# A spectral mixing block and a SwiGLU block in one kernel: which queues store the result, and in what pieces

## The chip, the cores and the metric

The kernel runs on one core of one Trainium2 chip. The metric is the device time of one execution in microseconds (us). Differences of about 0.3% are what a measurement of this kernel can tell from no change. All data are 32-bit floats.

## The reference

```python
batch, seq, dim = (8, 3008, 256)
X = np.fft.rfft(x, axis=1)
Y = X * (filt_r + 1j * filt_i)[None, :, :]
y = np.fft.irfft(Y, n=x.shape[1], axis=1)

x = y.reshape(B * S, D)                  # 24064 tokens of 256
g = x @ w_gate                           # 256 -> 1536
silu = g * (1.0 / (1.0 + np.exp(-g)))
val = x @ w_val
return silu * val @ w_out                # 1536 -> 256
```

The first block filters each channel along the sequence in the frequency domain. The second is a gated feed-forward network on every token. The weights come as 64-bit floats, which the kernel converts itself.

## The kernel before, in words

**Spectral block.** The Fourier transform of length 3008 = 47 x 64 is done as matrix products in two stages forward (`stage1`, and `stage2a` with the filter) and two back (`stage2b`, `stage3`). Intermediate results go through DRAM (`d1`, `d2`) and come back in another layout. The spectral work on batch b+1 runs in between the feed-forward work on batch b, in small pieces. Its tables, filters and inputs are loaded into a shared tile called `lent` and into tiles called `t4` (`t` in the profile). The matrix products are `pa`, `pb`, `pc` and `pd` by stage.

**Feed-forward block.** A batch is worked on in four chunks k = 0 to 3. The hidden units are split in three groups g = 0 to 2. One pair (k, g) is a step, a `Group` object, and takes about 25 us. The products use fewer multiplications than plain block products: a Toom-like scheme for the hidden layer (tokens P, Q, A, B, E, products `wk`, `wa`, `we`) and a Strassen-like scheme for the projection. The projection reads seven combinations of the hidden tiles `h`; four are made by GpSimd as sums (tokens S00 to S31, `h<-h` in the profile). GpSimd also makes differences such as D01 (`D<-f,f`), which VectorE combines further into the operands of later products (line 884, `wa<-wk,D`).

**Order of work.** One string, `SCHEDULE` (line 88), lists the tokens of a step in program order, and every engine and every queue executes its share in that order. A prime after a token means that it belongs to the step before, or, for projections and stores, to the one before that. The tokens `x0.o'` to `x5.o'` are the stores of a finished chunk. They stand at the beginning of a step, between S00/S01 and D01. The last chunk has a list of its own, `LAST` (line 99).

**The output tile.** The projection of a chunk is summed over the three groups in a tile `outs[b, k]` of 128 partitions, 16 rows and 96 columns, of which 94 hold data (`NR`); the two others are set to zero by GpSimd (line 824), so that VectorE can transpose whole 32 x 32 blocks (tokens z0 to z3, line 930). A chunk is then stored in twelve transfers (line 940), two to each token x0 to x5, each of up to 32 partitions with 16 pieces of 32 floats (128 bytes). SyncE's queue does this; in the last chunk SyncE and ScalarE take turns.

**The first batch.** Its first three chunks are taken in turns: all three with group 0, then with group 1, then with group 2, because the weights are still being converted (`takes_turns`, `order_of`). The tile of sums is therefore put away in DRAM (`o_dram`, line 935) after each of the first two groups and fetched again by `new_outs` (line 826); both move only the 94 columns with data. That is twelve transfers. The first batch also keeps and fetches `y` and its sums (`y_dram`, `yt_dram`), and stores and reloads the converted weights (`w_all`, lines 403 and 407).

**Queues.** Nearly all transfers are issued from SyncE's queue, in program order; ScalarE issues the stores of the spectral stages and half of the last chunk. GpSimd's queue issues no transfer.

Of the kernel before, what the change touches and what calls it, by code (L numbers as in the profile page):

```python
# [41 lines left out]
FP32 = mybir.dt.float32  # L42
# [6 lines left out]
B, S, C = 8, 3008, 256  # L49
# [6 lines left out]
NR = 2 * N1  # L56
NK = 4 * NS

NH = 4
# [3 lines left out]
RP = 96  # L63
NT = 3
NG = 3
# [31 lines left out]
KS = (-1, 0, 1, 2)  # L97

LAST = """
S00 S01 S10 S11 W1 o1 W2 o2 z0.o S20 S21 S30 S31 W6 o6 W5 o5 W3 o3 z1.o W7 o7 z3.o W4 o4 z2.o x0.o  # L100
x1.o x2.o x3.o x4.o x5.o
""".split()
BLOCKS = (0, 1, 3, 2)
PAIRS = ((0, 1), (1, 2), (2, 3), (0, 2), (1, 3), (0, 3))
# [68 lines left out]
def kernel(  # L173
# [10 lines left out]
    nc = tc.nc  # L184
# [9 lines left out]
    def pool(name, bufs, space=None):  # L194
        kw = {} if space is None else {"space": space}
        return ctx.enter_context(tc.tile_pool(name=name, bufs=bufs, **kw))
# [6 lines left out]
    wdpool = pool("wdram", 1, DRAM)  # L203
# [24 lines left out]
                  for i in range(4)]  # L228
    yt_dram = [wdpool.tile([128, 3 * len(PAIRS), TQ], FP32, name=f"yt_{k}") for k in range(NT)]
    y_dram = [wdpool.tile([128, 8, TQ], FP32, name=f"y_{k}") for k in range(NCHUNK)]  # L230
    o_dram = [wdpool.tile([128, 4 * NH, NR], FP32, name=f"o_{k}") for k in range(NT)]
    w_dram = wdpool.tile([NG, 128, NPR, 2, 128], FP32, name="w_all")
    wo_t = cpool.tile([128, NJ, 7, 128], FP32)

# [18 lines left out]
    pin = tc.keep_in_program_order  # L253

    def add(eng, dst, a, b):
        return eng.tensor_tensor(out=dst, in0=a, in1=b, op=ALU.add)  # L256
# [559 lines left out]
    outs = {}  # L816

    def takes_turns(b, k):
        return b == 0 and k < NT

    def new_outs(b, k, g):
        outs[b, k] = opool.tile([128, 4 * NH, RP], FP32, name=f"o_{b}_{k}_{g}", tag="o", bufs=2)
        if g == NG - 1 or not takes_turns(b, k):
            pin(nc.gpsimd.memset(outs[b, k][:, :, NR:], 0.0))
        if g:
            pin(nc.sync.dma_start(out=outs[b, k][:, :, 0:NR], in_=o_dram[k]))

    class Group:

# [93 lines left out]
        def project(self, op, last=False):  # L923

            b, k, q = self.b, self.k, self.g
            kind, p = op[0], int(op[1])
            if kind == "z":
                if q == NG - 1:
                    t = self.part(p)
                    pin(nc.vector.transpose(out=t, in_=t))  # L930
                return
            if kind == "x":
                t = outs[b, k]
                if q < NG - 1 and takes_turns(b, k) and p == 5:
                    pin(nc.sync.dma_start(out=o_dram[k], in_=t[:, :, 0:NR]))
                if q == NG - 1:
                    for n, (u, cq) in enumerate(divmod(m, 4) for m in (2 * p, 2 * p + 1)):
                        rows = min(32, NR - 32 * u)
                        at = (b * S + 32 * 32 * u + 2 * NH * k) * C + 32 * cq
                        pin(((nc.sync, nc.scalar)[n] if last else nc.sync).dma_start(  # L940
                            out=bass.AP(tensor=out.tensor, offset=out.offset + at,
                                        ap=[[32 * C, rows], [128, 4 * NH], [1, 32]]),
                            in_=t[32 * cq:32 * cq + rows, :, ts(u, 32)]))
                return
            at = {1: "A", 6: "A", 7: "A", 4: "A", 2: "F", 5: "G", 3: "G"}[p]
            if kind == "W":
                start = p in (1, 2, 5)
                if start:
                    self.bank(at, 3)
                for i in range(JB):  # L950
                    pin(nc.tensor.matmul(  # L951
                        out=self.tiles[at], lhsT=wo_t[:, JB * q + i, WO[p], :],
                        rhs=self.hs[i][:, HID[p]], start=start and i == 0,
                        stop=True, skip_group_check=True))
                return
            if q == 0 and p == 1:
                new_outs(b, k, q)
            i, cb = {1: (0, 0), 2: (0, 0), 6: (0, 1), 3: (0, 1), 4: (1, 0), 7: (1, 1),
                     5: (1, 1)}[p]
            dst = self.part(2 * i + cb)[:, :, 0:NR].rearrange("p n (t r) -> p t n r", t=2)  # L960
            src = self.tiles[at].rearrange("p (t n r) -> p t n r", t=2, n=NH)
            if q == 0 and at == "A":
                pin(nc.scalar.copy(out=dst, in_=src))
            else:
                pin(add(nc.vector, dst, dst, src))
# [7 lines left out]
    x0 = [t[0:NR, 8 * C * i:8 * C * i + 8 * C] for t, i in ((wo_f, 0), (wo_f, 1), (y_f, 0))]  # L973
    x0 = [t.rearrange("p (n c) -> p n c", c=C) for t in x0]
# [6 lines left out]
    with tc.tile_pool(name="start", bufs=1) as spool0:  # L981
# [12 lines left out]
        n = 0  # L994
# [68 lines left out]
        for p in ("A13", "A01"):  # L1063
            at = SLOT[p]
# [32 lines left out]
    def order_of(b):  # L1097

        steps = [divmod(step, NG) for step in range(NCHUNK * NG)]
        if b == 0:  # L1100
            steps[:NT * NG] = [(k, g) for g in range(NG) for k in range(NT)]
        return steps
# [39 lines left out]
    for step in range(NT, NT * NG):  # L1142
        chore(step, "Q3", lambda s: new_outs(0, *order_of(0)[s]), step)
# [4 lines left out]
    for b in range(B):  # L1148
# [36 lines left out]
        for step in range(NCHUNK * NG + (b == B - 1)):  # L1185
            ghost = step == NCHUNK * NG
            k, g = order_of(b)[min(step, NCHUNK * NG - 1)]
# [13 lines left out]
            last = ghost or b == B - 1 and step == NCHUNK * NG - 1  # L1201
            for place, token in enumerate(SCHEDULE):
# [5 lines left out]
                if op[0] == "t":  # L1208
                    n = int(op[1])
# [64 lines left out]
```

## Time and profile before

| | |
|---|---|
| time, median of three runs | 2918.26 us (2918.22 to 2924.73) |
| span of the profiled run | 2917.1 us |
| TensorE busy | 2850.2 us, 98% |
| VectorE busy | 2076.3 us, 71% |
| GpSimd busy | 1496.4 us, 51% |
| mean granted TensorE clock | 0.993 |
| stores to the result | 378 on SyncE's queue (first at 338.4 us), 6 on ScalarE's |
| kept sums, `o<-o` | 12 transfers, 752 KB each |

In the profile, PE is TensorE's matrix products, PEld its weight loads, DVE is VectorE, ACT ScalarE, POOL GpSimd, SP SyncE. "SPq" and "ACTq" are the queues on which SyncE and ScalarE issue transfers; the duration of such a line is that of the issues, not of the movement of data. A line of the timeline gives the start, the time, the engine, the line of code, the operation, the output and the inputs, and in square brackets the engine's idle time before it and what ended that. A line of the waits gives the waiting engine and its line, what it waited for, and then the total in us, the number of waits and the longest.

### The profile page before, as it was taken

The numbers are of one execution on the slowest core, as the hardware profiler recorded it, in microseconds if no ns is written. First come the engines' busy times: TensorE is split into PE (matmuls) and PEld (weight loads), VectorE is DVE, ScalarE is ACT, GpSimd is POOL, SyncE is SP. The second block draws the span as 40 slices with busy tenths as digits, with TensorE's granted clock in tenths as the row PEclk, the third lists the DMA queues.
The fourth block names the chain that finished last, engine by engine and source line by source line (L and its number), as shares of the span: only waits on it lengthen the run. The fifth ranks groups of instructions, "written<-read, shape, count | busy, mean of one in ns | idle before, by whom it ended". The sixth has DMA issues, their size and how long they took to land.

```text
span 2917.1 us, 47274 instructions
## 1 busy us (share of the span) xinstructions
PE 2850.2 (98%) x14784; PEld 2442.6 (84%) x14784; DVE 2076.3 (71%) x4664; ACT 1575.8 (54%) x4190; POOL 1496.4 (51%) x1613
## 2 busy tenths in 40 slices
PE   7999798999999999999999999999999999999998
PEld 6777687888888888888888888888888888888886
DVE  6888566767777676777677777676777776766666
ACT  6775344555555555555555555555555555555553
POOL 4876344545454545454544464545464545455442
PEclk9999999999999999999999999999999999999999
DMA  8799865666666766566656676566665666645443
GB/s 228 205 258 254 233 197 167 191 202 197 185 195 185 214 198 194 176 190 219 190 182 197 183 220 194 181 197 179 205 200 186 193 191 205 205 142 159 147 137 80
DMA packets 444350, 558.68 MB, mean 192 GB/s; under 512 B 251475, under 2 KB 346981, under 8 KB 444101
## 3 DMA queue, kind: packets, MB, share of 16 engines
q1 hardware_dynamic: 415349, 509.81, 59.1%
q10 hardware_dynamic: 28752, 45.85, 4.7%
q8 instruction: 120, 1.97, 0.3%
q14 instruction: 129, 1.06, 0.1%
HBM read 460.28 MB, written 95.24 MB: 190 GB/s over the span
## 4 chain that ended last, share of the span: by engine, by line
PE 86%; DVE 1%; DMA 1%; issue 0%; SPq 0%; DVEq 0%
PE wa L862 23%; PE wA L951 15%; PE wk L862 15%; PE we L862 12%; PE wG L951 8%; PE wF L951 3%; PE pd L765 3%; PE pc L731 2%; PE pb L698 2%; PE pa L639 1%; PE pa L641 1%; DMA t<-d 0%; DVE o L256 0%; DMA wt_t<-w_all 0%; DVE lent L714 0%
## 5 line engine op out<-in xcount | busy, mean ns | idle before, releaser
L862 PE MATMUL wa<-y_t,wt_t 128*128 128x188 f32 x4464 | 881.7, 324 | 6.8 <-DVE lent L714 1.7
L862 PEld LDWEIGHTS wa<-y_t,wt_t 128*128 128x128 f32 x4464 | 751.7, 191 | 87.5 <-ACT wa L888 9.1
L256 POOL TENSOR_TENSOR h<-h 128x376 f32<-128x376 f32 x190 | 184.5, 992 | 791.7 <-DVE h L909 791.7
L862 PEld LDWEIGHTS wk<-y,wt_t 128*128 128x128 f32 x2976 | 502.2, 190 | 79.9 <-DVE y L256 0.5
L862 PE MATMUL wk<-y,wt_t 128*128 128x188 f32 x2976 | 566.3, 323 | 0.0
L259 POOL TENSOR_TENSOR h<-h 128x376 f32<-128x376 f32 x570 | 563.3, 1010 | 0.0
L951 PE MATMUL wA<-h,wo_t 128*128 128x376 f32 x1536 | 548.8, 480 | 2.3 <-DVE o L256 1.6
L862 PE MATMUL we<-y_t,wt_t 128*128 128x188 f32 x2232 | 433.6, 324 | 0.8 <-ACT we L893 0.7
L259 DVE TENSOR_TENSOR we<-we,m 128x376 f32<-128x376 f32 x576 | 316.6, 554 | 142.7 <-PE we L862 94.0
L862 PEld LDWEIGHTS we<-y_t,wt_t 128*128 128x128 f32 x2232 | 371.3, 191 | 1.4 <-ACT we L893 1.0
L951 PEld LDWEIGHTS wA<-h,wo_t 128*128 128x128 f32 x1536 | 280.5, 190 | 106.5 <-DVE o L256 2.8
L259 POOL TENSOR_TENSOR D<-f,f 128x376 f32<-128x376 f32 x288 | 280.9, 987 | 149.4 <-ACT f L877 140.6
L897 ACT COPY m<-wa 128x376 f32<-128x376 f32 x576 | 271.7, 472 | 86.3 <-PE wa L862 83.3
L263 DVE SCALAR_TENSOR_TENSOR y<-wk,c 128x376 f32<-128x376 f32 x480 | 243.7, 540 | 84.9 <-ACT we L893 56.8
L904 ACT ACTIVATE u<-we 128x188 f32<-128x188 f32 x576 | 188.7, 328 | 190.0 <-DVE we L259 170.3
L904 ACT ACTIVATE g<-wa 128x188 f32<-128x188 f32 x576 | 187.3, 326 | 169.4 <-PE wa L862 153.4
L951 PE MATMUL wG<-h,wo_t 128*128 128x376 f32 x768 | 274.2, 479 | 1.2 <-DVE o L256 1.2
L877 ACT ACTIVATE f<-wk 128x376 f32<-128x376 f32 x288 | 139.2, 483 | 225.5 <-PE wk L862 159.5
L884 DVE SCALAR_TENSOR_TENSOR x<-wk,f 128x376 f32<-128x376 f32 x192 | 104.2, 543 | 214.0 <-PE wk L862 211.9
L881 ACT COPY c<-wk 128x376 f32<-128x376 f32 x288 | 136.0, 472 | 217.9 <-PE wk L862 217.9
L893 ACT COPY we<-y 128x376 f32<-128x376 f32 x480 | 221.2, 479 | 37.9 <-DVE h L909 24.7
L909 DVE TENSOR_TENSOR h<-wa,g 128x188 f32<-128x188 f32 x576 | 196.7, 345 | 34.3 <-ACT g L904 33.4
(156 smaller groups left out, 3822.1 us busy)
## 6 DMA issues: line engine op xcount, KB each, us to landing
wt_t<-w_all SPq DMA_DIRECT2D x174, 896.0 KB
wt_t<-w_all SPq DMA_DIRECT2D x174, 768.0 KB
lent<-later_tbl SPq DMA_DIRECT2D x84, 256.0 KB
lent<-in_filt_r_dram SPq DMA_DIRECT2D x336, 64.0 KB
d<-lent ACTq DMA_DIRECT2D x84, 256.0 KB
d<-t ACTq DMA_DIRECT2D x78, 240.0 KB
lent<-d SPq DMA_DIRECT2D x144, 128.0 KB
out_dram<-o SPq DMA_DIRECT2D x252, 64.0 KB
```

The source lines that it names most:

```text
L256: return eng.tensor_tensor(out=dst, in0=a, in1=b, op=ALU.add)
L259: return eng.tensor_tensor(out=dst, in0=a, in1=b, op=ALU.subtract)
L263: return nc.vector.scalar_tensor_tensor(out=dst, in0=a, scalar=-1.0, in1=b, op0=ALU.mult, op1=ALU.subtract)
L862: pin(nc.tensor.matmul(out=ps[:, z], lhsT=self.wt[:, SLOT[p], z], rhs=rhs, start=start and z == 0, stop=True, skip_group_check=True))
L877: pin(act.mul(self.small(f"f{i}", f"f{i}", 1), t[f"k{i}"], -1.0))
L881: pin(act.copy(out=self.small(f"c{i}", f"c{i}", 1), in_=t[f"k{i}"]))
L884: pin(v.scalar_tensor_tensor(out=dst, in0=t[f"k{j}"], scalar=-1.0, in1=t[f"f{i}" if j == 3 else f"D{at}"], op0=ALU.mult, op1=ALU.add))
L893: pin(act.copy(out=self.bank(f"e{at}"), in_=t[f"y{at}"]))
L897: pin(act.copy(out=self.small(f"m{at}", "m", 4), in_=t[f"a{at}"]))
L904: pin(act.activation(out=self.small(op, "g", 3, 1)[:, 0], in_=ps[:, 1], func=AF.Silu))
L909: pin(v.tensor_tensor(out=dst, in0=ps[:, 0], in1=g, op=ALU.mult))
L951: pin(nc.tensor.matmul(out=self.tiles[at], lhsT=wo_t[:, JB * q + i, WO[p], :], rhs=self.hs[i][:, HID[p]], start=start and i == 0, stop=Tru ...
```

## The change

It has three parts, all about moving the result. First, the stores of the first batch's chunks (b = 0) are issued from GpSimd's queue instead of SyncE's, so that SyncE's queue is left to the loads. Second, the sums that are put away between groups are moved as whole tiles of 96 columns, so that each partition is one contiguous piece in DRAM and in SBUF; the zero columns are then set once, at group 0, and travel with the tile. Third, the last chunk of all is stored in two halves: tokens x store the rows of the first half as soon as it is transposed, tokens X those of the second half at the end, and the transfers are dealt to SyncE, ScalarE and GpSimd in turn.

```diff
 LAST = """
-S00 S01 S10 S11 W1 o1 W2 o2 z0.o S20 S21 S30 S31 W6 o6 W5 o5 W3 o3 z1.o W7 o7 z3.o W4 o4 z2.o x0.o
-x1.o x2.o x3.o x4.o x5.o
+S00 S01 S10 S11 W1 o1 W2 o2 z0.o S20 S21 S30 S31 W6 o6 W5 o5 W3 o3 z1.o x0.o x1.o x2.o x3.o x4.o
+x5.o W7 o7 z3.o W4 o4 z2.o X0.o X1.o X2.o X3.o X4.o X5.o
 """.split()
...
-    o_dram = [wdpool.tile([128, 4 * NH, NR], FP32, name=f"o_{k}") for k in range(NT)]
+    o_dram = [wdpool.tile([128, 4 * NH, RP], FP32, name=f"o_{k}") for k in range(NT)]
...
-        if g == NG - 1 or not takes_turns(b, k):
+        if g:
+            pin(nc.sync.dma_start(out=outs[b, k], in_=o_dram[k]))
+        else:
             pin(nc.gpsimd.memset(outs[b, k][:, :, NR:], 0.0))
-        if g:
-            pin(nc.sync.dma_start(out=outs[b, k][:, :, 0:NR], in_=o_dram[k]))
...
-            if kind == "x":
-                t = outs[b, k]
+            if kind in "xX":
+                t, first, count = outs[b, k], 2 * NH * (kind == "X"), 2 * NH if last else 4 * NH
                 if q < NG - 1 and takes_turns(b, k) and p == 5:
-                    pin(nc.sync.dma_start(out=o_dram[k], in_=t[:, :, 0:NR]))
+                    pin(nc.sync.dma_start(out=o_dram[k], in_=t))
                 if q == NG - 1:
                     for n, (u, cq) in enumerate(divmod(m, 4) for m in (2 * p, 2 * p + 1)):
                         rows = min(32, NR - 32 * u)
-                        at = (b * S + 32 * 32 * u + 2 * NH * k) * C + 32 * cq
-                        pin(((nc.sync, nc.scalar)[n] if last else nc.sync).dma_start(
+                        at = (b * S + 32 * 32 * u + 2 * NH * k) * C + 128 * first + 32 * cq
+                        queue = nc.sync if b else nc.gpsimd
+                        if last:
+                            queue = (nc.sync, nc.scalar, nc.gpsimd)[(2 * p + n) % 3]
+                        pin(queue.dma_start(
                             out=bass.AP(tensor=out.tensor, offset=out.offset + at,
-                                        ap=[[32 * C, rows], [128, 4 * NH], [1, 32]]),
-                            in_=t[32 * cq:32 * cq + rows, :, ts(u, 32)]))
+                                        ap=[[32 * C, rows], [128, count], [1, 32]]),
+                            in_=t[32 * cq:32 * cq + rows, first:first + count, ts(u, 32)]))
```

## The prediction, made before the changed kernel was timed

> **What bounds the kernel now.** I read the page's head first, then busy time by stretches, then TensorE's waits, then the timeline of one step of the first batch and of the end.
>
> ```profile
> span 2917.1 us, 47274 instructions
> PE 2850.2 (98%) x14784; PEld 2442.6 (84%) x14784; DVE 2076.3 (71%) x4664; ACT 1575.8 (54%) x4190; POOL 1496.4 (51%) x1613
> ```
>
> TensorE sets the time. What can be gained lies where it is idle, and the stretches show where:
>
> ```profile
> 300.00:400.00 100.00, 85.35 (x409) 72.35 (x409) 66.73 (x143) 40.98 (x111) 44.98 (x47) 0.93 0.81 225
> 400.00:500.00 100.00, 87.19 (x435) 75.18 (x434) 58.64 (x133) 43.68 (x118) 43.10 (x45) 0.93 0.55 167
> 500.00:600.00 100.00, 100.00 (x524) 86.39 (x523) 71.97 (x164) 55.36 (x148) 45.89 (x48) 1.00 0.63 190
> ```
>
> The columns are the stretch, its length, and the busy time of PE, PEld, DVE, ACT and POOL, then granted clock, DMA share and GB/s. From 500 us to 2890 us TensorE is idle for 2 us in all. From 300 to 500 us it is idle for 14.65 + 12.81 = 27.5 us, and its clock records there hold 27.3 us at half speed, so 13.7 us more. About 41 us are to be had there. What ends the idle time:
>
> ```profile
> PE pb L698 <- DMA lent<-d: 11.9, 5, 8.4
> ...
> PE pd L765 <- DMA t<-d: 9.9, 1, 9.9
> ```
>
> These are loads on SyncE's queue. The timeline of the step that begins near 330 us (chunk 2, third group of hidden units) shows why one of them came late, and what GpSimd does meanwhile:
>
> ```profile
> 330.45 1.92 POOL L256 TENSOR_TENSOR h<-h 128x376 f32<-128x376 f32 x2 [11.20 <-DVE h L909]
> ...
> 336.20 0.99 POOL L259 TENSOR_TENSOR D<-f,f 128x376 f32<-128x376 f32 x1
> ...
> 338.38 10.12 SPq L940 DMA_DIRECT2D out_dram<-o  x12
> ...
> 339.25 0.55 DVE L884 SCALAR_TENSOR_TENSOR wa<-wk,D 128x376 f32<-128x376 f32 x1
> ...
> 352.56 0.37 SPq L407 DMA_DIRECT2D wt_t<-w_all  x1
> ...
> 359.59 0.39 SPq L530 DMA_DIRECT2D lent<-d  x1
> ...
> 362.48 2.05 PE L698 MATMUL pb<-lent 128*128 128x256 f32 x4 [8.43 <-DMA lent<-d]
> ```
>
> SyncE's queue issues the twelve stores of chunk 0 for 10.1 us; the weight reload and the load that TensorE waits for (the last line but one) stand behind them. In the built program a transfer on SyncE's or ScalarE's queue waits for the landing of the one eight places before it, so a slow one blocks all behind it. GpSimd makes the Strassen sums (`h<-h`) and then D01, which VectorE uses 2 us after it is done.
>
> ```profile
> 2909.45 0.58 DVE L930 STREAM_TRANSPOSE o<-o 128x384 f32<-128x384 f32 x1
> 2910.06 3.21 SPq L940 DMA_DIRECT2D out_dram<-o  x6
> 2910.06 3.34 ACTq L940 DMA_DIRECT2D out_dram<-o  x6
> ```
>
> At the end, all twelve stores wait for the last transpose; 7 us pass from there to the end of the span.
>
> **What the Trainium skill says.** "DMA: Bandwidth & Descriptors", SWDGE vs HWDGE vs iDMA: a DMA issued by GpSimd has its descriptors computed by cores of GpSimd itself. The trace before has none, so cannot agree or differ. The same page, Why small descriptors are slow: each packet carries a fixed overhead. The trace agrees: its 376-byte packets took 42 ns on average, its 6144-byte ones 298 ns, 7 times as long for 16 times the bytes. "TensorE: Matmul & The Clock Gate", What's actually happening: an idle window of about 3.4 us halves the clock. The trace agrees: after the idle 8.43 us it records half clock for 10.24 us, after 9.89 us again 10.24 us, after 2.76 us 3.41 us.
>
> **Part 1, stores of the first batch from GpSimd.** Removed: 48 issues from SyncE's queue (10.1, 10.3, 8.0 and 6.6 us of it in the steps of chunks 0 to 3) and 48 places in its chain of eight. Added: 48 issues on GpSimd, in its order. The built program shows where: behind the first sums `h<-h` come eight stores, a sum of the spectral stage, two stores, the second sums, two stores, and then D01. So D01 comes 12c later, c being one issue, and the second sums 10c later. The wait for the transposes costs nothing: z1 ends at 332.2 us, the first sums at 332.4 us.
>
> Who waits: VectorE for D01, and TensorE behind it. The room is best read in a step in which no DMA disturbs (chunk 3):
>
> ```profile
> 514.37 0.98 POOL L259 TENSOR_TENSOR D<-f,f 128x376 f32<-128x376 f32 x1 [0.88 <-ACT f L877]
> ...
> 517.86 0.54 DVE L884 SCALAR_TENSOR_TENSOR wa<-wk,D 128x376 f32<-128x376 f32 x1
> ...
> 520.36 1.44 PE L862 MATMUL wa<-y_t,wt_t 128*128 128x188 f32 x8
> ```
>
> D01 ends at 515.35 us, VectorE takes it 2.5 us later, its result is done at 518.40 us and TensorE reads it at 520.36 us, 2.0 us on. With the 0.88 us that GpSimd waited itself, 5.4 us; in the other steps 0.6 to 0.7 us of waiting, or none, and 2.0 to 2.6 us to VectorE. I take 5.0 us. The stall is 12c - 5.0 per chunk, four times.
>
> c is not in the trace. Lower end: SyncE's own issue of such a store, 0.48 us, or 0.62 us, which "SBUF — State Buffer" (A bandwidth-pool intuition that's wrong) gives for a GpSimd DMA alone; upper end 3.1 us, its price beside a VectorE copy that holds the port. The DMA page (Latency and other measured facts) has about 1 us to the first byte. Our stores have 512 pieces of 128 bytes; SyncE takes 0.48 us for one and 0.39 us for a load of 128 rows, 1.25 times less. I take 1.0 x 1.25 = 1.25 us, an estimate.
>
> Then a stall is 12 x 1.25 - 5.0 = 10.0 us, and four are 40.0 us. Such idle times cost half clock for 10.24 us, 5.1 us each: 20.5 us. Against this stand the 41 us of 300 to 500 us: with SyncE's queue free by 8 to 10 us and TensorE later by 10 us, the loads arrive before they are needed. The load for `pd` hangs partly on transfers that follow TensorE, so I leave 5 us of loss: -36.0 us. Part 1: 40.0 + 20.5 - 36.0 = +24.5 us.
>
> **Part 2, kept sums in whole tiles.** Twelve transfers (six out, six back) change from 2048 packets of 376 bytes to 128 of 6144: 12 x 2048 x 42 ns / 16 engines = 64.5 us become 12 x 128 x 298 ns / 16 = 28.6 us, 36 us less of DMA between 138 and 361 us. TensorE waits little for DMA before 300 us (1.4 us for x); the rest is in the 41 us already. The moved memsets (three of 0.13 us) lie in GpSimd's gaps, the padding columns add 2% to the bytes. I take -1.5 us.
>
> **Part 3, the last chunk in halves.** The first half's data are ready at 2906.6 us, before TensorE's last products, so its issues hide there. The second half then has four issues a queue instead of six: two of some 0.5 us fewer on SyncE and ScalarE, about -1.1 us. GpSimd has 8c for half the pieces, from 2906.6 us: at 1.0 us it issues until 2914.6 us, 1.2 us after today's last issue (2913.4 us), at 0.6 us earlier than the others. Between -1.2 and +2.5 us; I take -1.0 us.
>
> Sum: 24.5 - 1.5 - 1.0 = +22.0 us, 2940 us.
>
> **The rivals.** *Cheap issue, c = 0.62 us:* stalls of 2.4 us, 9.8 us in four, with 1.7 us of clock each 16.6 us; 16.6 - 36.0 - 2.5 = -22 us, 2896 us. For it: the published time for a DMA alone, SyncE's 0.48 us, and VectorE mostly reading PSUM here. Against: 512 pieces a store.
> *It cancels, c = 0.9 us:* stalls of 5.8 us, 23.2 us, clock 3.4 us each, 13.6 us; less 38.5 us makes -2 us, 2917 us. It needs c in a narrow band.
> *Dear issue, c = 2 us or more:* stalls of 19 us, 76 us, with clock 24 us, less 39 us: +61 us, 2979 us; with 3.1 us about 3032 us. For it: 512 pieces on two cores. Against: nothing in the trace; the published times are shorter.
>
> **How the numbers follow.** Forecast 0.40, cheap 0.33, cancels 0.17, dear 0.10. Faster by over 0.3% (8.8 us) is the cheap case, 0.33; within 0.3% the third, 0.17; slower the forecast and the dear case, 0.50. The range runs from 2894 us (the cheap case) to 2972 us (c near 1.8 us); outside are the dear case and a cheaper issue than I bound.
>
> **What would show it.** GpSimd's issues spaced by 1.25 us behind the first sums; TensorE waiting for VectorE or GpSimd some 10 us in the steps near 335, 380, 415 and 515 us, the last of them new in a stretch that was full; the 8.43 us and most of the 9.89 us wait gone; 6144-byte packets for the kept sums. It is wrong if GpSimd's issues are spaced under 0.9 us, if its sums run on while descriptors are made, or if the loads stay late with SyncE's queue free.

## The result, and the profile after

The changed kernel takes 2895.51 us (median of four runs, 2894.28 to 2897.16) against 2921.49 us before (the three runs of the table above and one more, 2925.41 us): a ratio of 0.9911, 95% interval 0.9894 to 0.9928. It was forecast to be 22 us slower; it is 26 us faster. Measured twice more, beside the experiments, the ratio was 0.9931 (0.9918 to 0.9943) and 0.9927 (0.9915 to 0.9940).

The head of the page of the changed kernel, and the same stretches as before:

```profile
span 2893.4 us, 47312 instructions
PE 2843.6 (98%) x14784; PEld 2434.4 (84%) x14784; DVE 2073.4 (72%) x4664; ACT 1576.6 (54%) x4190; POOL 1532.2 (53%) x1669
```

```profile
300.00:400.00 100.00, 91.17 (x451) 75.34 (x451) 71.04 (x155) 44.86 (x119) 65.04 (x77) 1.00 0.81 258
400.00:500.00 100.00, 95.24 (x497) 80.92 (x496) 63.60 (x150) 51.78 (x139) 59.94 (x69) 1.00 0.55 169
500.00:600.00 100.00, 100.00 (x530) 87.06 (x529) 71.78 (x166) 57.16 (x151) 43.93 (x46) 1.00 0.60 183
```

TensorE's idle time from 300 to 500 us has gone from 27.5 to 13.6 us, and the clock column reads 1.00 instead of 0.93: none of the 13.7 us that half clock cost is left. What is left of the waits has other causes. TensorE's waits from 300 to 500 us:

```profile
PE wa L862 <- DVE wa L884: 5.6, 4, 1.4
PE wA L954 <- POOL h L259: 4.6, 4, 2.5
...
PE pb L698 <- DMA lent<-d: 0.9, 1, 0.9
```

The waits of 8.43 and 9.89 us for loads are gone. The first two lines are new: four times TensorE waits for GpSimd's second sums, and four times for the operand that VectorE makes from D01, 10.2 us together. The timeline of the step of chunk 2, third group, shows the order that the prediction read from the built program:

```profile
323.92 5.34 POOL L943 DMA_DIRECT2D out_dram<-o  x8
...
330.49 1.41 POOL L943 DMA_DIRECT2D out_dram<-o  x2
331.92 1.95 POOL L259 TENSOR_TENSOR h<-h 128x376 f32<-128x376 f32 x2
...
332.96 1.86 PE L954 MATMUL wA<-h,wo_t 128*128 128x376 f32 x4 [0.38 <-POOL h L259]
...
335.21 0.99 POOL L259 TENSOR_TENSOR D<-f,f 128x376 f32<-128x376 f32 x1
...
336.85 1.54 PE L862 MATMUL wa<-y_t,wt_t 128*128 128x188 f32 x8 [1.39 <-DVE wa L884]
```

Eight issues take 5.34 us, 0.667 us each. The line of all stores on GpSimd's queue says the same (the shortest, the median and the longest issue in ns):

```profile
L943 POOL DMA_DIRECT2D out_dram<-o x56: 597/651/836, 323.9 to 2889.3; - x56
```

The eight issues at the end of the kernel, of 256 pieces each, are among the 56. The end of the kernel:

```profile
2883.79 5.27 SPq L943 DMA_DIRECT2D out_dram<-o  x8
2883.80 5.35 ACTq L943 DMA_DIRECT2D out_dram<-o  x8
...
2886.62 0.58 DVE L930 STREAM_TRANSPOSE o<-o 128x384 f32<-128x384 f32 x1
2887.49 2.43 POOL L943 DMA_DIRECT2D out_dram<-o  x4 [0.98 <-DVE o L930]
```

From the end of the last transpose to the end of the span it is 2893.4 - 2887.2 = 6.2 us; before it was 2917.1 - 2910.0 = 7.1 us.

**Where the time came from.** All of these kernels run the same 4653 arithmetic instructions and transposes on VectorE, and all but `e6_later` (in which 99 stand at other places) in the same order, so the start of one and the same instruction can be compared between two traces. The changed kernel's lead over the kernel before, by the time at which an instruction starts in the trace before (all times from the start of each trace's span):

| start before, us | 216 | 229 | 302 | 337 | 379 | 460 | 518 | 564 | 2753 |
|---|---|---|---|---|---|---|---|---|---|
| lead of the changed kernel, us | -0.2 | 1.5 | 3.0 | 8.7 | 17.5 | 25.7 | 21.1 | 22.9 | 22.8 |

The lead grows where the waits for loads were. It dips in the steps with stores on GpSimd (not in the table: 6.2 us at 353, 11.7 us at 393), and shrinks by 2.8 us for good in the step of chunk 3 (460 to 564 us), a stretch that was full before. It then stays to the end.

### The profile page after: what moved, and what is told of

Same layout as the page of the kernel before. It is cut to its first block, busy times and chain, and to the rows that moved or that the text cites. A ratio compares the mean times of both kernels' runs of the same rounds, so it can differ in the third digit from the quotient of the medians.

```text
span 2893.4 us, 47312 instructions
## 1 busy us (share of the span) xinstructions
PE 2843.6 (98%) x14784; PEld 2434.4 (84%) x14784; DVE 2073.4 (72%) x4664; ACT 1576.6 (54%) x4190; POOL 1532.2 (53%) x1669
## 4 chain that ended last, share of the span: by engine, by line
PE 89%; POOL 3%; DVE 2%; issue 1%; ACT 0%; DMA 0%; POOLq 0%; DVEq 0%
PE wa L862 24%; PE wA L954 16%; PE wk L862 15%; PE we L862 12%; PE wG L954 8%; PE wF L954 4%; PE pd L765 3%; PE pc L731 3%; PE pb L698 2%; PE pa L639 1%; PE pa L641 1%; POOL out_dram L943 1%; POOL h L259 1%; POOL h L256 0%; DVE o L256 0%
```

## The experiments

Theory A: the gain is part 1, SyncE's queue freed of the stores, and the prediction went wrong in the price of an issue on GpSimd and nothing else. Rival B: the gain is part 2, the shorter kept sums. Rival C: GpSimd's sums don't wait for its issues, so that these cost nothing at all. Each ratio below is against the kernel before on the same chip.

**Part 1 alone** (`e1_stores`).

```diff
-                        pin(((nc.sync, nc.scalar)[n] if last else nc.sync).dma_start(
+                        queue = nc.sync if b else nc.gpsimd
+                        pin(((nc.sync, nc.scalar)[n] if last else queue).dma_start(
```

> The kernel before with part 1 alone: the first batch's stores from GpSimd's queue. If the gain comes from SyncE's queue being free of the stores, nearly all of it is here: 0.992 to 0.994 of the time before (some 18 to 23 us less), GpSimd's issues spaced by 0.67 us as in the changed kernel, and the 8.4 and 9.9 us waits of TensorE gone. If the gain comes from the shorter transfers of the kept sums instead, this is within 8 us of the time before, or slower for the added issues on GpSimd.

2911.0 us, ratio 0.9965 (0.9953 to 0.9977): 10 us less, half of what theory A expected. An issue took 0.66 us. The long waits for loads are gone, as expected; but the trace is 6 us behind the kernel before at 229 us, where no store has run yet (one run; the run with part 3 alone, which has the same first batch as the kernel before, was 2.0 us behind there), and waits of up to 3.6 us for loads remain. TensorE's waits for them from 130 to 600 us:

```profile
PE pa L658 <- DMA x<-in_x_dram: 4.1, 2, 3.6
...
PE pb L698 <- DMA lent<-d: 3.6, 3, 1.5
```

**Part 2 alone** (`e2_sums`): the `o_dram`, `new_outs` and store lines of the change, nothing else.

> The kernel before with part 2 alone: kept sums as whole tiles. The prediction's share was -1.5 us; the two traces drift apart by about 3 us up to 320 us, before the first store, so I expect 2 to 4 us less and the waits at 354 and 441 us still there. The rival, that these transfers delayed the loads, expects 12 us or more.

2909.5 us, ratio 0.9963 (0.9951 to 0.9976): 11 us less, near the 12 us or more of rival B and far from the 2 to 4 us of theory A. Yet the long waits stand; TensorE's waits from 130 to 600 us in this run:

```profile
PE pd L765 <- DMA t<-d: 9.6, 1, 9.6
PE pb L698 <- DMA lent<-d: 9.3, 1, 9.3
```

So neither theory holds alone. The two parts gain about 10 us each by different waits: this trace gains 5.7 us on the kernel before from 302 to 337 us, where short waits and 3.4 us at half clock are gone, and stays near 8 us ahead from 353 us on.

**Part 3 alone** (`e3_tail`).

> The kernel before with part 3 alone: last chunk in two halves from three queues. From the last transpose to the end of the span it is 7.1 us before and 6.2 us in the changed kernel, so about 1 us less, 0.9997 of the time before. If GpSimd's issue at the end cost as much as 1.25 us, it would be 1 to 2 us more.

2919.38 us, ratio 0.9996 (0.9988 to 1.0004). The interval contains no change; the number is near the 0.9997 expected. The three ratios multiply to 0.9924, inside the interval of the whole change.

**Twice as many issues on GpSimd** (`e4_double`).

```diff
+                        parts = 1 if b else 2
+                        for h in range(parts):
+                            f, c = first + h * count // parts, count // parts
...
-                                ap=[[32 * C, rows], [128, count], [1, 32]]),
+                                            ap=[[32 * C, rows], [128, c], [1, 32]]),
```

> The changed kernel with each store of the first batch cut into two, so 24 issues on GpSimd for a chunk, of 256 pieces each (0.61 us an issue, as at the end of the changed kernel). If the prediction's sum was right but for the size of one issue, the delay is 24 x 0.61 = 14.6 us, the stall of TensorE 9 to 10 us a chunk instead of about 3, and half clock comes back: 30 to 45 us more than the changed kernel, 2925 to 2940 us. If GpSimd's sums don't wait for its issues, or have much more room than 5 us, it is within 5 us of the changed kernel.

2930.9 us, ratio 1.0035 (1.0023 to 1.0046): slower than before, and 35 us above the changed kernel's 2895.5 us; 4 us of that the profiled run had lost already at 130 us, before any store. Rival C falls. TensorE's waits from 300 to 600 us, and the step of chunk 2 in the timeline:

```profile
PE wA L957 <- POOL h L259: 28.5, 4, 8.0
```

```profile
328.11 9.42 POOL L946 DMA_DIRECT2D out_dram<-o  x16
337.55 1.27 POOL L256 TENSOR_TENSOR lent<-lent 128x512 f32<-128x512 f32 x1
338.75 2.50 POOL L946 DMA_DIRECT2D out_dram<-o  x4
341.27 1.92 POOL L259 TENSOR_TENSOR h<-h 128x376 f32<-128x376 f32 x2
342.31 2.87 PE L957 MATMUL wA<-h,wo_t 128*128 128x376 f32 x4 [6.67 <-POOL h L259]
```

Twenty issues stand ahead of the second sums, 9.42 + 2.50 = 11.9 us; TensorE waits 28.5 / 4 = 7.1 us a chunk for these sums, and another 3.9 us in all for the operand made from D01. Half clock is back: 37.5 us of it from 300 to 600 us, which costs 18.8 us. An issue of 256 pieces took 9.42 / 16 = 0.59 us against 0.667 us for 512.

**No stores of the first batch** (`e5_no_stores`); this kernel leaves the rows of batch 0 unwritten.

```diff
-                if q == NG - 1:
+                if q == NG - 1 and b:
```

> The changed kernel without the 48 stores of the first batch: the rows of batch 0 are not written, nothing else is left out. It shows what the stores still cost where they are. In the changed kernel TensorE waits 10.2 us for GpSimd's sums and for VectorE's operand made from D01 between 300 and 500 us, and falls back 2.8 us in the step of chunk 3. If these waits are the price of the issues, this is 8 to 13 us less than the changed kernel. If the waits for loads come back in their place, it is within 3 us of it.

2880.51 us, ratio 0.9874 (0.9861 to 0.9888), beside 0.9931 (0.9918 to 0.9943) for the changed kernel on the same chip: 16 us less by the medians, 13.9 us by the spans of the profiled runs (2879.3 and 2893.2 us). That is what the stores still cost in the changed kernel, 3.5 to 4 us a chunk. The stretches:

```profile
300.00:400.00 100.00, 97.63 (x495) 82.93 (x494) 78.77 (x169) 49.82 (x133) 56.00 (x57) 1.00 0.76 257
400.00:500.00 100.00, 100.00 (x535) 87.38 (x535) 68.50 (x163) 56.47 (x152) 41.27 (x44) 1.00 0.53 169
```

No wait for a load came back in place of those for GpSimd, but for the 1.1 us for `lent` that the changed kernel has too (0.9 us).

**All stores later in the step** (`e6_later`): tokens x0 to x5 behind S31 in `SCHEDULE`, for all batches.

```diff
-                ... S30' t1.2 x02 W7 S31' g13 y12 ...
+                ... S30' t1.2 x02 W7 S31' x0.o' x1.o' x2.o' x3.o' x4.o' x5.o' g13 y12 ...
-        chore(step, "Q3", lambda s: new_outs(0, *order_of(0)[s]), step)
+        chore(step, "E03", lambda s: new_outs(0, *order_of(0)[s]), step)
```

> The changed kernel with tokens x0 to x5 moved behind S31, where GpSimd has made all sums of the step, and with the fetch of the next tile of sums moved from Q3 to E03, so that SyncE doesn't stand waiting for these stores. If the remaining price is the place of the issues in GpSimd's order, it comes near the kernel without the stores: 6 to 12 us less than the changed kernel. The rival: the later stores hold the tile of sums or the loads, waits for transfers return, and nothing or less is gained.

2912.48 us, ratio 0.9983 (0.9975 to 0.9991): a miss as a kernel, but its trace is split in two. At 564 us its lead over the kernel before was 33.9 us (36.2 us without stores); at the end 10.0 us. It fell back 3 to 6 us at each of five places, near 875, 1230, 1579, 1938 and 2295 us of its own trace, in the later batches, where SyncE's stores had moved too. The trace shows what they held up. VectorE's waits from 600 to 2880 us have a line that the changed kernel's lack:

```profile
DVE paired L259 <- DMA x<-in_x_dram: 26.6, 8, 6.4
```

These are loads of the next batch's input on SyncE's queue. At four of the five places VectorE waits 5.3 to 6.4 us for one of them, and ScalarE and then TensorE wait behind VectorE, TensorE 2.7 to 3.6 us. How the moved stores made these loads late was not followed.

**Only the first batch's stores later** (`e8_first_later`): the same place on GpSimd for b = 0, the old place on SyncE for the others.

```diff
-        chore(step, "Q3", lambda s: new_outs(0, *order_of(0)[s]), step)
+        chore(step, "E03", lambda s: new_outs(0, *order_of(0)[s]), step)
...
+                    if old and op == "S31" and older is not None and older.b == 0:
+                        for p in range(6):
+                            older.project(f"r{p}.o")
```

> The changed kernel with the first batch's stores alone moved behind S31 on GpSimd, the other batches' stores left where they were, and the next tile of sums fetched at E03. The run with all stores moved kept pace with the kernel without stores up to 530 us and lost 24 us later, where SyncE's stores of the later batches had moved too. If that loss comes from the later batches, this one keeps the lead: 9 to 14 us less than the changed kernel, within 4 us of the kernel without stores. If not, it falls back as that run did.

2886.28 us (2881.88 to 2890.16), ratio 0.9898 (0.9883 to 0.9914), beside 0.9927 (0.9915 to 0.9940) for the changed kernel on the same chip: 9 us less. In the profiled runs it is 36.1 us ahead of the kernel before at 2753 us, as far as the kernel without stores, though it still makes the 48 transfers. That profiled run is the fastest of four; by the two ratios it is some 7 us short of the kernel without stores. TensorE's waits from 300 to 600 us hold nothing of the second sums or D01 any more:

```profile
PE pc L731 <- POOL lent L256: 1.7, 1, 1.7
PE pb L698 <- DMA lent<-d: 1.1, 1, 1.1
```

This version is faster than both kernels. The stores' place and that of the fetch changed together; no run has one without the other.

**The stores from ScalarE's queue** (`e7_scalar`): `nc.scalar` in place of `nc.gpsimd` for the first batch.

> The changed kernel with the first batch's stores from ScalarE's queue. These are again part of the chain of eight transfers, and ScalarE must issue them between its activations: 12 x 0.48 us a chunk if it never waits, more where the chain holds it. If the point of GpSimd's queue is that its transfers are outside the chain, this is 8 us or more slower than the changed kernel. If any queue but SyncE's does, it is within 4 us of the changed kernel or faster, since an issue takes 0.48 instead of 0.65 us.

2903.14 us, ratio 0.9950 (0.9937 to 0.9964), 7 us slower than the changed kernel on that chip, between the two expectations. TensorE's waits show what ScalarE's issues delay:

```profile
PE wk L862 <- ACT f L877: 16.4, 5, 4.8
```

ScalarE's own negated copies `f` come late. Whether the chain of eight or the issues themselves held ScalarE isn't settled by this run; issues took up to 1.6 us. GpSimd's transfers are not free of such a chain either: in the built program of the changed kernel they take eight semaphores of their own in turn, but GpSimd waited on it only once, 0.7 us.

**Kept sums in 94 columns, rows of 96 in DRAM** (`e9_rows`, from the changed kernel, and `e10_pitch`, from the kernel before).

```diff
-            pin(nc.sync.dma_start(out=outs[b, k], in_=o_dram[k]))
+            pin(nc.sync.dma_start(out=outs[b, k][:, :, 0:NR], in_=o_dram[k][:, :, 0:NR]))
...
-                    pin(nc.sync.dma_start(out=o_dram[k], in_=t))
+                    pin(nc.sync.dma_start(out=o_dram[k][:, :, 0:NR], in_=t[:, :, 0:NR]))
```

> The changed kernel with the kept sums moved in 94 columns again, 376 bytes a piece, but with rows of 96 columns in DRAM. If part 2 gains by its long pieces, this is 8 to 13 us slower than the changed kernel, as the run with part 2 alone was faster by 11 us. If the gain came from anything else (the order of the memsets, the place in DRAM), it is within 4 us of the changed kernel.

2897.35 us, ratio 0.9931 (0.9918 to 0.9943): 1.6 us slower than the changed kernel (0.9927), well within the intervals. The long pieces are not what part 2 gains by. Packets of 376 bytes in the records of the three traces, mean ns in the six transfers out and the six back:

| | out, mean ns | back, mean ns |
|---|---|---|
| before, rows of 376 bytes in DRAM | 46 to 68 | 22 to 24 |
| `e9_rows`, rows of 384 bytes | 23 to 30 | 22 to 24 |
| `e10_pitch`, rows of 384 bytes | 24 to 33 | 22 to 24 |

The pieces have the same length; those written at a pitch of 376 bytes take twice as long and more. The kernel before with the pitch alone changed was the test:

> The kernel before with one thing changed: rows of 96 columns instead of 94 for the kept sums in DRAM; 94 columns are moved as before, in pieces of 376 bytes. In the traces, packets of 376 bytes written to rows 376 bytes apart take 46 to 68 ns on average in each of six transfers, those read back 23 ns, and written to rows 384 bytes apart 23 to 30 ns. If the pitch of the rows is what part 2 gains by, this gives what part 2 alone gave, 8 to 12 us less than before. If it is the length of the pieces, it is within 3 us of the time before.

2908.71 us, ratio 0.9968 (0.9956 to 0.9980): 9 us less where part 2 alone gave 11, with overlapping intervals and packets no longer than before. What the slow writes held up is SyncE's queue, on which each transfer waits for one eight places earlier. Its waits for kept sums to land, from 130 to 600 us, in the kernel before and then in `e10_pitch`:

```profile
SPq L530 <- DMA o<-o: 14.4, 3, 5.9
SPq L826 <- DMA o<-o: 4.3, 1, 4.3
...
SPq L530 <- DMA o<-o: 2.9, 3, 2.0
SPq L826 <- DMA o<-o: 1.8, 1, 1.8
```

Together 18.7 us became 4.7 us (0.8 us with part 2 alone). Why rows 376 bytes apart are written so slowly is not shown; only these two pitches were run.

## Why the prediction was wrong

**What bounds the kernel** held: in the changed kernel the time moved between 216 and 525 us and by 0.9 us at the end, nowhere else.

**The step that failed is "I take 1.0 x 1.25 = 1.25 us, an estimate"**, the price c of an issue on GpSimd. It measured 0.65 to 0.67 us, near the "0.62 us" that was the lower end, from "SBUF — State Buffer"; that page gives it for a whole DMA alone, not for an issue, so the closeness of the two is no confirmation. No issue came near the 3.1 us of the upper end; the longest took 0.84 us. Two things were wrong in it: I took the time to the first byte as the issue's own time, and let it grow with the 512 pieces as SyncE's issue does. GpSimd's barely grows: 0.59 us for 256 pieces, 0.667 us for 512. The rival "cheap issue" had nearly this number, and its 2896 us was the result to 0.5 us. Its change was 4 us off, though: -22 us against the measured -26, since it was reckoned from 2918 us, and the median before became 2921.49 us with the fourth run. With c = 0.667 us and no half clock the prediction's own sum makes 12.0 - 36.0 - 2.5 = -26.5 us, but that agreement is luck in its parts, as follows.

**The stall "12c - 5.0 per chunk"** was about right. With 0.667 us it gives 3.0 us, 12 us in four; the kernel without stores puts the price at 13.9 to 16 us. With 24 issues at 0.59 us it gives 9.2 us a chunk, and TensorE waited (28.5 + 3.9) / 4 = 8.1 us. There most of it was for the second sums, in the changed kernel nearly half (4.6 of 10.2 us): the prediction named both and reckoned with D01 alone.

**Half clock, "5.1 us each",** came with stalls of 7 us (in the run with double issues) and not at all in the changed kernel, whose stalls of 3 us are split into waits of at most 2.5 us. So the size of c counted twice, and the cheap rival's 1.7 us each was too much. It was a near thing: 3.4 us of half clock followed single waits of 2.4 us in `e10_pitch`, 2.76 us in the kernel before and 3.5 us in `e9_rows`, so these traces give no sharp limit.

**"-36.0 us" for part 1** was right as a pool of what loads cost, wrong as part 1's own. Without stores, and with parts 2 and 3, the lead is 36.1 us. Part 1 alone gained 10 us net of the stalls, and 9.8 us of waits for loads stood in its trace from 130 to 600 us: `pa` and `pb` as shown, and 2.1 us for `y_t`.

**Part 2, "I take -1.5 us",** was 9 to 11 us when made alone. The step "TensorE waits little for DMA before 300 us" looked at TensorE alone and left the rest to the 41 us that part 1 was to win, while SyncE's queue, in which the later loads stand, waited 18.7 us for the kept sums to land. Its mechanism was wrong too: the prediction leant on "DMA: Bandwidth & Descriptors", Why small descriptors are slow, and took the length of the packets for the cause. The trace had the means to see it: the reads of the same length took 23 ns, so the "42 ns" that it said to agree with the page is an average of two directions and shows no cost of short packets as such.

**Part 3, "-1.0 us",** was right in size (0.9 us in the profile) though too small for its interval. So the cheap rival reached the right sum with a part 2 too small and a part 1 too large.

## What to carry to other kernels

Before a transfer is put on a busy engine's queue, measure the issue there, and count what of that engine's work stands behind it in program order; put it after the last work that another engine waits for. That place, with the fetch moved along, was worth 9 us more here, a third of the whole gain again. Where a tile is kept in DRAM, look at the duration of the packets in each direction apart: a row of 94 floats that became 96 gave 9 of the 11 us that the whole tiles gave.

## What the runs showed that I had not expected

An issue on GpSimd took 0.65 to 0.67 us for 512 pieces of 128 bytes, only 0.08 us more than for 256, against 0.48 us in the median on SyncE; from issue to landing it was 4.0 us in the median (2.0 to 7.5). Packets of 376 bytes written to DRAM at a pitch of 376 bytes took 46 to 68 ns, at 384 bytes 23 to 33 ns, and reads at either pitch 22 to 24 ns. Moving SyncE's stores of the later batches by a quarter of a step cost 24 us, most of it by waits of VectorE for the next batch's input; how the moved stores made these loads late stays open.
